# Last stage of the gated convolutions on shared weight loads, two channel groups at a time, in a new order

## The chip, the core and the metric

The kernel runs on one core of one Trainium2 chip. The metric is the device time of one execution in microseconds. Three runs of the kernel before took 241.77, 242.07 and 239.66 us, so its median is 241.77 us. One more execution was profiled; all rows quoted here come from that one.

## The reference

Two long convolutions over 2048 positions and 448 channels are mixed by a gate. `u` is the input, and both convolutions are causal (the reference takes them by FFT over the padded length).

```
x = A_u                                                   # [1, 2048, 448]
g = sigmoid(sum(x * gate_w, -1))                          # one number per position
K = Re sum_n C[d,n] * exp(dt[d] A[d,n] l) * dt[d] B[d,n]  # 2048 taps per channel, 256 modes
a = causal_conv(x, K) + x * Dskip
k_shift = 4-tap causal convolution of B_k
kv = k_shift * B_v
b = x * (causal_conv(kv, ssm_k) + kv * ssm_D)             # the gated convolution
out = g * a + (1 - g) * b
```

Inputs and output are bf16. The kernel folds both skip terms (`Dskip`, `ssm_D`) into the first tap of the convolution kernels.

## The kernel before, in words

**Layout.** The 448 channels are 4 groups of 112. A position is 64·a + b with a below 32 and b below 64, and the 128 partitions are (group, a). So a tensor in natural order is 128 partitions by 64 values of b by 112 channels. `natv` (called `vt`, later `ug`) first holds `v`, then k_shift·v, and at the end the output; `natu` (called `uu`) holds the shifted copy of `k` for the taps and then `u`, which arrives by four DMAs on the SP queue after the taps are done.

**Stages.** The 112 channels are worked in four windows H = 0..3 of 28 (`NC`). A convolution of one window is a chain of matrix products in TensorE, each leaving PSUM through ScalarE or VectorE:

- `spread` (matmuls with `Wc` or `WcK`) and `transform` (matmuls with 32 matrices of `s2_W`): the forward transform of the data and of the taps;
- `swapped`: eight DMAs on SP that exchange the two halves of the partitions of one factor, for the complex product;
- `products`: two VectorE multiplications of 128x3584;
- `stage_a` (matmuls with `R`): first stage of the inverse, evacuated as `U` of shape [2, 64, 28] into a slot;
- `stage_b` (matmuls with `G`): the last stage. For each of the 64 values of b and each of two terms r it loads a 128x128 slice of `G` and multiplies it with `U[:, r, b]`, 28 columns; the two terms add up in PSUM. 32 values of b fill one piece of two PSUM banks, which is then consumed.

**Order of calls.** `PLAN` says in which order the parts are written down. `B` is a window of the gated convolution (`conv_B`), `T` makes the taps of a window of the other one (`table`: `exps` and `levels` with exponentials and sines on ScalarE, then `tables` of VectorE products, `sums` on TensorE, `gather`, `spread`), `A` is a window of the other convolution (`conv_A`), and `m` is a VectorE pass over a finished window (`mix`). `A` of window 0 has its own `stage_b`; windows 1, 2 and 3 share one `stage_b` of 84 columns in six pieces at the end of the kernel (`epilogue`: a gated multiplication out of PSUM, an addition, the stores).

**How the last stage of a `B` window is consumed.** For windows 0, 1 and 2 `epilogue_B` multiplies each of two pieces out of PSUM with the window of `u` on VectorE and writes `ug`. For window 3 `held` copies the two pieces to `ug` by `evac`, and the pass `("m", 3)` multiplies the window with `u` afterwards. The pass `("m", 0)` adds the two finished convolutions of window 0.

**Resources.** `places.slots` are eight SBUF slots of 128x3584 bf16, handed out in the order of the digits of `SLOTS`; `places.joint(n)` hands out n at once as one tile. `places.room()` hands out one of four PSUM rooms of two banks by the digits of `ROOMS`. `evac` takes the next letter of `SIDES`: V evacuates with VectorE, S with ScalarE; there are 265 letters, 57 of them V.

**What sets the order.** All calls are recorded, 6102 of them, and `Order.issue` emits them in the order of the list `ORDER`, with an ordering dependency from each instruction to the one before it on its engine. So the order on each engine and on the SP and POOL queues is written out by hand; every recorded instruction is therefore put down to the same line, L131, of the profile, and the groups are told apart by their tiles (`q` are the slots, `ps` the PSUM rooms, `TP` and `TQ` the tables).

Of the kernel before, what the change touches and what calls it, by code (L numbers as in the profile page):

```python
# [36 lines left out]
PLAN = (("T", 0), ("B", 0), ("B", 1), ("T", 1), ("B", 2), ("A", 0), ("T", 2), ("B", 3), ("A", 1), ("T", 3), ("A", 2), ("m", 0), ("m", 3), ("A", 3))  # L37
PIECES = (12, 12, 12, 12, 12, 4)
SLOTS = (
    "0434052127765603307644115551700367426427537106156704014032"  # L40
)
ROOMS = (
    "01233232320132033030321023302112031100122001132032113022220031322311020231103030220220312330023120301132132010331031"
    "3231321320202123101203132012012212012323303012030110320011003102201222120212310132310321"
)
SIDES = (
    "SSSSVSVSVSSSSSSSSSSVVVVVVSSVSSSSVSVSSSSSSSSSSSSSSSSSSVVSSSVSSSVSSSSSVSSSSSSSSSVSSSSVVSVSVSVSVVVVVVVSSSSSSSSSSSSSSSSS"
    "SSSSSSSSSSSSSSSSSSSSSVSSSSSSSSSSVVSVSVSSVVVSSSSSSSSSSSSSSSSSSSSSSSSSSSSSSSSSSSSSSSSSSSSSSVVVVVVSVVVSVSSVVSSSVSSSVSSS"
    "SSSSSSSSSVSSSSSSSSSSSVVSSSSVSSSSV"
)  # L50
ORDER = (
# [277 lines left out]


def stage_b(nc, places, G, U, consume, less=None, pieces=(32, 32), w=NC):
    per = 512 // w if w > NC else 16
    b0 = 0
    for n in pieces:
        pt = places.room()
# [605 lines left out]
```

## Time and profile before

| what | us |
|---|---|
| median of three runs | 241.77 |
| the profiled execution, whole | 242.85 |
| its span, first to last instruction | 241.1 |
| VectorE (DVE) busy in it | 216.2 |
| ScalarE (ACT) busy in it | 195.1 |
| TensorE matmuls (PE) busy | 199.7 |
| TensorE weight loads (PEld) busy | 187.1 |

The profile's groups give busy time, the count behind an x, the mean ns of one instruction, and the idle time of the engine just before with what ended it. A busy time of matmuls counts each from its start to its modelled end, and they overlap; the mean of a matmul is therefore longer than the distance from one to the next. In the view by windows, each engine has the busy time in the stretch and the number of instructions. In the timeline a row is a run of like instructions: start, duration of the run, engine, kind, tiles, count, and in brackets the idle time before it and what ended it.

### The profile page before, as it was taken

Reading aid. Unit: us, or ns where it says so; the run is one execution under the profiler, and the core shown is the slowest. Engines: PE = TensorE matmul, PEld = TensorE weight load, DVE = VectorE, ACT = ScalarE, POOL = GpSimd, SP = SyncE. Lnnn points to the kernel's source line nnn. Section 1 sums busy time; section 2 is a strip of 40 time slices with the busy share of each in tenths; the row PEclk is TensorE's granted clock in tenths of the full one; section 3 lists DMA queues with packets and bytes.
Section 4 is the critical chain, followed back from the end, with each engine's and each line's share of the span. In section 5 each row is a group of like instructions: output and inputs, shape, how many; then the busy total and the mean of one; then the engine's idle time right before and its main releaser. Section 6 shows DMA issues by size and latency. Waiting matters only on the chain.

```text
span 241.1 us, 11786 instructions
## 1 busy us (share of the span) xinstructions
PE 199.7 (83%) x5358; PEld 187.1 (78%) x5358; DVE 216.2 (90%) x316; ACT 195.1 (81%) x260; POOL 22.2 (9%) x34
## 2 busy tenths in 40 slices
PE   1701988899978996999999999989999999799930
PEld 1501887898867996998999999989999899689720
DVE  1999999998987996999899999999999999977790
ACT  2899976998986986799999999988999998449000
POOL 9400001110000020100000012000121120000000
PEclk9999999999999999799999999999999999979995
DMA  6999999989384699641506047142175373500195
GB/s 142 217 182 203 153 185 315 194 192 203 61 141 93 158 176 218 145 96 31 127 8 120 3 79 137 21 97 63 22 155 102 79 132 94 129 5 3 34 175 98
DMA packets 64865, 28.86 MB, mean 120 GB/s; under 512 B 54960, under 2 KB 63280, under 8 KB 64688
## 3 DMA queue, kind: packets, MB, share of 16 engines
q1 hardware_dynamic: 57904, 21.69, 43.9%
q0 software_dynamic: 2160, 5.51, 12.6%
q10 hardware_dynamic: 4752, 0.92, 2.1%
q8 instruction: 42, 0.69, 1.3%
q14 instruction: 7, 0.06, 0.1%
HBM read 10.41 MB, written 2.75 MB: 55 GB/s over the span
## 4 chain that ended last, share of the span: by engine, by line
DVE 31%; PE 23%; DMA 8%; SPq 6%; issue 5%; ACT 3%; DVEq 0%
PE ps L131 23%; DVE TQ L131 11%; DVE TP L131 10%; SPq L131 6%; DVE q L131 4%; DMA natu<-in_A_u_dram 4%; ACT q L131 3%; DVE natv L131 3%; DVE natu L131 2%; DMA TP<-TP 2%; DMA q<-q 2%; DVE RK L131 1%; DVE ET L131 0%; ACT RK L131 0%; DVEq L131 0%
## 5 line engine op out<-in xcount | busy, mean ns | idle before, releaser
L131 ACT CAST q<-ps 128x1024 bf16<-128x1024 f32 (+3 forms) x158 | 132.8, 936 | 15.6 <-PE ps L131 11.2
L131 PEld LDWEIGHTS <-q 128*128 128x128 bf16 (+3 forms) x944 | 60.7, 143 | 21.6 <-DVE q L131 11.8
L131 PE MATMUL ps<-small,q 128*128 128x128 bf16 (+2 forms) x688 | 45.2, 240 | 13.3 <-DMA natv<-in_B_v_dram 11.4
L131 DVE TENSOR_TENSOR TQ<-TQ,ET 128x896 bf16<-128x896 bf16 (+2 forms) x70 | 45.8, 685 | 0.2
L131 PE MATMUL ps<-TP,TQ 128*32 128x32 bf16 x1792 | 33.9, 241 | 5.6 <-issue 3.7
L131 PEld LDWEIGHTS <-TQ 128*32 128x32 bf16 x1792 | 30.7, 155 | 8.0 <-issue 5.2
L131 PE MATMUL ps<-q,s_W 128*128 128x112 bf16 (+1 forms) x544 | 32.2, 211 | 2.3 <-DVE natv L131 1.9
L131 DVE TENSOR_TENSOR q<-q 128x3584 bf16<-128x3584 bf16 (+1 forms) x22 | 32.4, 1511 | 1.9 <-ACT q L131 0.8
L131 PEld LDWEIGHTS <-natu 128*32 128x32 bf16 (+1 forms) x560 | 28.5, 183 | 4.5 <-issue 3.8
L131 DVE TENSOR_TENSOR TP<-TP,ET 128x1792 bf16<-128x1792 bf16 (+3 forms) x25 | 31.5, 1271 | 0.0
L131 PEld LDWEIGHTS <-G 128*128 128x128 bf16 x768 | 28.7, 117 | 2.3 <-DVE q L131 0.7
L131 PEld LDWEIGHTS <-s_W 128*128 128x128 bf16 x544 | 26.9, 98 | 4.7 <-issue 3.0
L131 PE MATMUL ps<-q,G 128*128 128x28 bf16 (+1 forms) x768 | 29.9, 186 | 0.5 <-ACT q L131 0.5
L131 POOL DMA_DIRECT2D TP<-TP x15 | 13.1, 893 | 147.3 <-issue 41.6
L131 ACT ACTIVATE q<-hold 128x448 bf16<-128x448 f32 (+1 forms) x48 | 22.7, 534 | 0.1
L131 ACT ACTIVATE ET<-q 128x1344 bf16<-128x1344 int16 (+1 forms) x12 | 17.5, 1469 | 0.1
L131 PE MATMUL ps<-q,natu 128*32 128x336 bf16 (+3 forms) x336 | 15.0, 289 | 2.4 <-ACT q L131 2.1
L131 ACT CAST RK<-ps 128x448 bf16<-128x448 f32 (+1 forms) x16 | 12.0, 762 | 6.0 <-PE ps L131 6.0
L131 DVE CAST q<-ps 128x896 bf16<-128x896 f32 (+4 forms) x14 | 12.8, 918 | 3.5 <-PE ps L131 3.3
L131 PE MATMUL ps<-small,natu 128*64 128x128 bf16 x224 | 15.5, 284 | 0.3 <-DVE natv L131 0.3
L131 PE MATMUL ps<-small,natv 128*64 128x128 bf16 x224 | 15.2, 285 | 0.3 <-ACT q L131 0.3
L131 DVE TENSOR_TENSOR TQ<-TQ 128x448 bf16<-128x448 bf16 (+2 forms) x35 | 15.3, 445 | 0.1
(63 smaller groups left out, 197.5 us busy)
## 6 DMA issues: line engine op xcount, KB each, us to landing
q<-q SPq DMA_DIRECT2D x64, 112.0 KB, 3.4
TP<-TP POOLq DMA_DIRECT2D x9, 448.0 KB, 5.7
q<-in_B_ssm_k_dram SPq DMA_DIRECT2D x16, 112.0 KB, 3.8
natv<-in_B_v_dram SPq DMA_DIRECT2D x4, 448.0 KB, 7.3
natu<-in_A_u_dram SPq DMA_DIRECT2D x4, 448.0 KB, 6.9
TP<-TP POOLq DMA_DIRECT2D x6, 224.0 KB, 4.5
s_W<-c_W SPq DMA_DIRECT2D x1, 1024.0 KB, 6.5
G<-c_G SPq DMA_DIRECT2D x4, 256.0 KB, 5.2
```

What stands on the lines that cost most here:

```text
L131: ins = f(*args, **kw)
```

## The change

- `conv_B` no longer ends in its own `stage_b`. An even window takes two slots as one tile (`places.joint(2)`), and `inverse` writes its `U` into the first half; the odd window writes the second half, and then one `stage_b` serves both windows: 64 values of b times two terms, 56 columns each, in four pieces of 16 values of b.
- `epilogue_B` now takes each piece of both windows: it multiplies 2 x 8 x 56 columns out of PSUM with `u` and writes `ug`, for windows (0, 1) and (2, 3) alike. `held` and the pass `("m", 3)` are gone.
- `per` in `stage_b` is rounded down to an even number (8 for 56 columns; 84 columns keep 6).
- `ORDER`, `SLOTS`, `ROOMS` and `SIDES` are new throughout. There are 5845 calls (256 fewer matmuls and one pass fewer); `SIDES` has 263 letters, 54 of them V.

```diff
-PLAN = (..., ("A", 2), ("m", 0), ("m", 3), ("A", 3))
+PLAN = (..., ("A", 2), ("m", 0), ("A", 3))
 ...
 def stage_b(nc, places, G, U, consume, less=None, pieces=(32, 32), w=NC):
-    per = 512 // w if w > NC else 16
+    per = 512 // w // 2 * 2 if w > NC else 16
 ...
-    def epilogue_B(H):
-        def consume(b0, n, pt):
-            o = window(ug, b0, n, H).rearrange("p (i b) c -> p i b c", b=16)
-            x = window(uu, b0, n, H).rearrange("p (i b) c -> p i b c", b=16)
-            V.tensor_tensor(out=o, in0=pt.rearrange("p i (b c) -> p i b c", b=16), in1=x, op=ALU.mult)
-        return consume
-
-    def held(t, H):
-        def consume(b0, n, pt):
-            evac(window(t, b0, n, H).rearrange("p (i b) c -> p i b c", b=16), pt.rearrange("p i (b c) -> p i b c", b=16))
-        return consume
+    def epilogue_B(b0, n, pt, H):
+        o, x = (t[:, b0:b0 + n, H * NC:(H + 2) * NC].rearrange("p (i b) c -> p i b c", i=2) for t in (ug, uu))
+        V.tensor_tensor(out=o, in0=pt.rearrange("p i (b c) -> p i b c", c=2 * NC), in1=x, op=ALU.mult)
 ...
+    pair = []
+
     def conv_B(H):
 ...
-        conv(products(nc, K, S, X), epilogue_B(H) if H < NQG - 1 else held(ug, H))
+        terms = products(nc, K, S, X)
+        if H % 2 == 0:
+            pair.append(places.joint(2).rearrange("p h (r b c) -> p h r b c", r=2, b=64))
+        inverse(pair[-1][:, H % 2], terms)
+        if H % 2:
+            U = pair[-1]
+            stage_b(nc, places, G, lambda r, b: U[:, :, r, b], lambda b0, n, pt: epilogue_B(b0, n, pt, H - 1), None, (16,) * 4, 2 * NC)
 ...
-        V.tensor_tensor(out=o, in0=o, in1=x, op=ALU.mult if H else ALU.add)
+        V.tensor_tensor(out=o, in0=o, in1=x, op=ALU.add)
```

The new `ORDER` also moves work that the change does not touch. On VectorE the two products of `A` window 1 and the pass `("m", 0)` stand behind the last of the `tables` instructions now, and stood ahead of it. On SP the eight swaps of `B` window 1 stand ahead of all four loads of `u`; before, two of these loads stood ahead of the swaps and two behind them. On ScalarE three of window 2's sine passes stand between its exponentials now; before, they stood ahead of them.

More of the change, by code (lines that the diff above doesn't have):

```diff
@@ L36 @@
 NSLOT = 8
-PLAN = (("T", 0), ("B", 0), ("B", 1), ("T", 1), ("B", 2), ("A", 0), ("T", 2), ("B", 3), ("A", 1), ("T", 3), ("A", 2), ("m", 0), ("m", 3), ("A", 3))
+PLAN = (("T", 0), ("B", 0), ("B", 1), ("T", 1), ("B", 2), ("A", 0), ("T", 2), ("B", 3), ("A", 1), ("T", 3), ("A", 2), ("m", 0), ("A", 3))
 PIECES = (12, 12, 12, 12, 12, 4)
 SLOTS = (
-    "0434052127765603307644115551700367426427537106156704014032"
+    "0410735562045402302751323214026032471666553507656744714032"
 )
 ROOMS = (
-    "01233232320132033030321023302112031100122001132032113022220031322311020231103030220220312330023120301132132010331031"
-    "3231321320202123101203132012012212012323303012030110320011003102201222120212310132310321"
+    "10323210022103031313223213113030130032021113302022131210020033201030102011022311031022311322113002011230212303213131"
+    "1211020111123310003322233202012211013101110020323203020011123120312301233130303220313202"
 )
 SIDES = (
-    "SSSSVSVSVSSSSSSSSSSVVVVVVSSVSSSSVSVSSSSSSSSSSSSSSSSSSVVSSSVSSSVSSSSSVSSSSSSSSSVSSSSVVSVSVSVSVVVVVVVSSSSSSSSSSSSSSSSS"
-    "SSSSSSSSSSSSSSSSSSSSSVSSSSSSSSSSVVSVSVSSVVVSSSSSSSSSSSSSSSSSSSSSSSSSSSSSSSSSSSSSSSSSSSSSSVVVVVVSVVVSVSSVVSSSVSSSVSSS"
-    "SSSSSSSSSVSSSSSSSSSSSVVSSSSVSSSSV"
+    "VVSVSSVSVSSSSSSSSSSSSSVVVVSVVVSSSSVSSSSSSSSSSSSSSSSSSSVSSSSSSSSSSSSSVVVSSSSSSSVSSSSVVVVVVSSSSVSSVVSSSSSSSSSSSSSSSSSS"
+    "SSSSSSSSSSSSSSSSSVSSSSSSSSSVVVSVVVVVVSSVVVSSSSSSSSSSSSSSSSSSSSSSVSSSSSSSSSSSSSSSSSSVSSVSSSSSVSSVSVSSVSSSSSSSVSVSSSSS"
+    "SSSSSSSSSSSSSSSSSSSSVSVSVSSSVVS"
 )
 ORDER = (
[46 rows of a table removed]
[46 rows of a table added]
 )
```

92 rows, old and new, of the table ORDER are left out of this document.

## The prediction

> **What bounds the kernel now.** I read the page first, then busy time by stretches, then the waits of VectorE, then the timelines at the places where VectorE stood still, and last the groups by shape.
>
> ```profile
> span 241.1 us, 11786 instructions
> PE 199.7 (83%) x5358; PEld 187.1 (78%) x5358; DVE 216.2 (90%) x316; ACT 195.1 (81%) x260; POOL 22.2 (9%) x34
> ...
> core 0: us, PE busy (x) PEld busy (x) DVE busy (x) ACT busy (x) POOL busy (x), PEclk, DMA share, GB/s
> 0.00:20.00 20.00, 4.98 (x48) 4.45 (x48) 14.34 (x24) 14.32 (x23) 8.29 (x17) 1.00 0.89 180
> 20.00:55.00 35.00, 29.10 (x712) 27.45 (x712) 34.43 (x50) 30.48 (x43) 2.72 (x3) 1.00 1.05 208
> 55.00:116.00 61.00, 55.19 (x1517) 51.95 (x1517) 54.53 (x69) 52.65 (x68) 2.60 (x3) 0.97 0.68 133
> 116.00:205.00 89.00, 86.61 (x2478) 81.55 (x2470) 87.79 (x145) 86.23 (x116) 8.57 (x11) 1.00 0.40 81
> 205.00:235.00 30.00, 23.85 (x624) 21.67 (x624) 25.14 (x31) 11.44 (x16) 0.00 (x0) 0.94 0.33 69
> ...
> 98.00:198.00 100.00, 97.13 (x2753) 92.13 (x2754) 97.99 (x152) 97.51 (x132) 8.57 (x11) 1.00 0.40 83
> ```
>
> VectorE is the bound. From 20 to 55 us it lacks 0.6 us, from 116 to 205 us 1.2 us. It is idle only from 55 to 116 (6.5 us) and in the tail from 205 (4.9 us). ScalarE is as full as VectorE from 98 to 198. TensorE looks as full, but its busy time holds overlapped latencies, as the pricing below shows. Who makes VectorE wait between 55 and 116:
>
> ```profile
> DVE natv L131 <- DMA natu<-in_A_u_dram: 2.6, 1, 2.6
> DVE TQ L131 <- PE ps L131: 2.4, 2, 2.2
> ...
> 73.86 0.62 DVE L131 TENSOR_TENSOR TQ<-hold,ET 128x896 bf16<-128x896 bf16 x1 [2.25 <-PE ps L131]
> ...
> 92.66 2.09 DVE L131 TENSOR_TENSOR natv<-ps,natu 128x896 bf16<-128x896 f32 x2 [2.59 <-DMA natu<-in_A_u_dram]
> ...
> 203.39 1.83 DVE L131 TENSOR_TENSOR TQ<-TQ,ET 128x448 bf16<-128x448 bf16 x5
> ...
> 234.32 0.68 DVE L131 TENSOR_TENSOR natv<-natu,natv 128x1008 bf16<-128x1008 bf16 x1
> ```
>
> Two holes hold 4.8 of the 6.5 us: at 71.6 the first table product of window 1 waits for TensorE to finish reading the tables of window 0, and at 90.1 the last stage of `B` window 0 waits for `u`. The last two rows mark the tail: the last table instruction ends at 205.2, the last VectorE instruction at 235.0. The span then needs 6.1 us for the stores.
>
> **The change part by part.** Everything is priced by these groups:
>
> ```profile
> L131 ACT CAST q<-ps 128x896 bf16<-128x896 f32 x64 | 56.1, 933 | 10.3 <-PE ps L131 6.7 <-DVE natv L131 3.5
> ...
> L131 DVE TENSOR_TENSOR q<-q 128x3584 bf16<-128x3584 bf16 x14 | 27.9, 2019 | 1.7 <-ACT q L131 0.8 <-issue 0.5 <-DVE q L131 0.3
> ...
> L131 PE MATMUL ps<-q,G 128*128 128x28 bf16 x640 | 23.3, 183 | 0.0
> ...
> L131 PE MATMUL ps<-q,G 128*128 128x84 bf16 x128 | 6.6, 201 | 0.5 <-ACT q L131 0.5
> ...
> L131 DVE TENSOR_TENSOR natv<-ps,natu 128x896 bf16<-128x896 f32 x6 | 6.4, 1086 | 2.6 <-DMA natu<-in_A_u_dram 2.6
> ...
> L131 ACT ACTIVATE q<-hold 128x224 int32<-128x224 f32 x16 | 6.1, 415 | 0.0
> L131 DVE TENSOR_SCALAR q<-hold 128x224 int32<-128x224 f32 x23 | 6.0, 306 | 0.0
> ...
> L131 DVE CAST q<-ps 128x896 bf16<-128x896 f32 x4 | 4.3, 1081 | 0.1
> ...
> L131 DVE TENSOR_TENSOR natv<-natv,natu 128x1792 bf16<-128x1792 bf16 x2 | 2.2, 1086 | 0.0
> ...
> L131 ACT CAST natv<-ps 128x896 bf16<-128x896 f32 x2 | 2.0, 1019 | 0.0
> ...
> L131 ACT ACTIVATE ET<-ET 128x672 bf16<-128x672 bf16 x2 | 1.6, 790 | 0.5 <-DVE ET L131 0.5
> ...
> L131 ACT COPY q<-ps 128x224 f32<-128x224 f32 x4 | 1.2, 335 | 0.0
> ```
>
> *TensorE.* Today a last-stage matmul of 28 columns with its weight load costs 23.3/640 = 36.4 ns of busy time, one of 84 columns 6.6/128 = 51.6 ns. Shape 56 is not in the trace, and lies halfway: between 36.4 and 51.6, I take 44. Before, 512 x 36.4 = 18.6 us; after, 256 x 44 = 11.3 us. TensorE loses 7.4 us (5.4 to 9.3). Since it is not the bound, this does not shorten the path by itself; it only lets TensorE be ready earlier. A price of twice 36.4, at which nothing is shared, is excluded by the row of 84 columns.
>
> *VectorE.* Two windows now leave by four products of 896 out of PSUM; over the kernel there are eight instead of six, +2 x 1.09, and the pass over window 3 goes, -1.09: +1.1 us. The writes go to 56 adjacent columns instead of 28; I keep 1.09.
>
> *ScalarE.* The two copies of window 3 go, -2.0 us.
>
> *The letters.* I laid the letters of `SIDES`, old and new, beside the calls that take them. Until the end of the tables VectorE gets two transforms (2 x 1.08) and two short copies, and gives away two casts of `spread` and `stage_a`, five phases and two negations; successive VectorE instructions overlap by about 0.08 us, and net of that it is some -0.7 us. Behind the tables it gets three casts (two of `stage_a`, one of `gather`) and gives one away: +2.0. ScalarE loses four large casts in all, the two of window 3 among them (4 x 0.95 = -3.8), and two short copies (-0.7), and gets the five phases (5 x 0.42 = +2.1) and two negations (2 x 0.79 = +1.6): -0.8 us.
>
> *A cost that the diff does not name.* ScalarE reloads its function table whenever exponentials and sines alternate:
>
> ```profile
> L131 ACT ACT_TABLE_LOAD x6 | 7.7, 1283 | 1.3 <-PEq L925 1.2
> ...
> 158.62 1.28 ACT L131 ACT_TABLE_LOAD   x1
> 159.91 1.32 ACT L131 ACTIVATE ET<-q 128x1344 bf16<-128x1344 int16 x1
> ```
>
> The new order puts window 2's three sine passes between its exponentials, so there are eight loads instead of six: +2 x 1.28 = +2.6 us, right in the stretch where ScalarE has 2.5 us left in 100. Nothing hides them there. ScalarE ends at -0.8 + 2.6 = +1.8 us. (The Trainium skill, "ScalarE: Activation LUTs", section "What ACT_TABLE_LOAD costs", adds a drain of about 1.38 us to each switch; by it the two would cost 5.3 us. The trace differs: the sine starts 0.01 us behind the load, so the row decides.)
>
> *The end of the tables.* Ahead of that point VectorE loses the products of `A` window 1 (2 x 2.0 less overlap, -3.9) and the pass over window 0 (-1.0 net), both moved behind it, gains two last-stage products (+2.0 net) and loses 0.7 by letters: -3.6 us. These 3.9 and 1.0 are only moved.
>
> *The hole at 90.1.* What the SP queue does before it:
>
> ```profile
> 77.47 4.51 SPq L131 DMA_DIRECT2D q<-q  x6
> 82.02 3.22 SPq L131 DMA_DIRECT2D natu<-in_A_u_dram  x2
> ```
>
> The last loads of `u` are issued at 82 to 85 because six swaps of `B` window 1 stand ahead and wait for that window's transforms, which TensorE reaches late. In the new order these transforms are early, the swaps follow those of window 0 directly, and the first consumer of `u` on VectorE stands some 9 us of VectorE work later. I take the full 2.6 us as gained (0 if the swaps, whose last pieces wait for a cast on VectorE, hold the queue again).
>
> *The hole at 71.6.* Between the end of window 0's tables and the last read of them, TensorE has three runs of eight `transform` matmuls fewer in the new order,
>
> ```profile
> 85.98 0.57 PE L131 MATMUL ps<-q,s_W 128*128 128x112 bf16 x8
> ```
>
> at up to 0.57 us each, so up to 1.7 us; VectorE has 0.4 us more of its own work in the same stretch. Of the hole 0 to 2.1 us are gained; I take the middle, 1.1.
>
> *New waits.* One is visible, in the second half of window 3's tables:
>
> ```profile
> 192.44 2.08 DVE L131 TENSOR_TENSOR TP<-TP,ET 128x1792 bf16<-128x1792 bf16 x2
> ...
> 201.09 1.08 DVE L131 TENSOR_TENSOR TP<-TP,q 128x1792 bf16<-128x1792 bf16 x1
> ```
>
> The second row needs what a DMA on the POOL queue sums up behind the first, and starts 6.6 us after it ends; in the new order 4.2 us of VectorE work lie between the two. I put 0.6 us (0 to 1.5, as the wait need not show at all or may take most of the missing 2.4). One slot of eight is held from window 2's `stage_a` to window 3's last stage; whatever waits for slots I cannot price and leave to the range.
>
> *The tail.* Its 25.1 us of VectorE work gain the two products (+3.9), the casts (+2.0) and the pass over window 0, and lose the pass over window 3: 31.1. Some of the 4.9 us idle is filled by this, the chain sums, `gather`, `spread`, transform, product, `stage_a` still has to run: between 31.1 and 36.0, I take 33, +3.0.
>
> *Sum*, against the profiled execution: 242.85 - 3.6 - 2.6 - 1.1 + 0.6 + 3.0 = 239.15, which is -3.7 us. The runs' median lies 1.1 us under that execution: 241.77 - 3.7 = **238.1 us**. With all bounds at their good end -3.6 - 2.6 - 2.1 + 1.1 = -7.2 (234.6); all at the bad end, -3.6 + 1.5 + 6.0 = +3.9 (245.7); they hardly meet all at one end, and 234.5 to 241.5 is this case's own range.
>
> **Rivals.**
>
> *No change: the evacuating engines set the pace.* VectorE's total rises (1.1 - 0.7 + 2.0 = 2.4 us) and ScalarE's by 1.8. If closed holes reappear as waits elsewhere and only the one for `u` stays closed, 241.77 + 2.4 - 2.6 = 241.6; with none closed 244.2. For it: 97.99 and 97.51 of 100 us. Against: 11 us of idle time are there to be taken. (The Trainium skill, "Perfetto Trace Analysis", section "Identifying the Most-Contended Engine", says to work on the engine with the highest occupancy and not to trust matmul busy time; here that is VectorE with 90%, and the change takes nothing from it. The trace agrees as to matmul time.)
>
> *TensorE was the bound after all.* It is also busy 97.13 of those 100 us. Then the 7.4 us come off whole: 234.4. Against: 36 ns per matmul where one lasts 183.
>
> *Slower: results wait for VectorE in PSUM.* Two of eight pieces could leave by ScalarE before; now all need VectorE, in its written order, and each keeps one of four rooms until then:
>
> ```profile
> 82.97 2.29 PE L131 MATMUL ps<-q,G 128*128 128x28 bf16 x64
> ```
>
> This piece was complete at 85.3 and stood until 92.66: 7.4 us. If TensorE runs out of rooms because of it, ScalarE runs dry with it, and has no slack to catch up. At one instruction of 1.09 us per piece, eight pieces cost 8.7 us: 238.1 + 8.7 = 246.8. It decides from the fourth blocked piece on, where the 3.7 us are eaten. For it: four pieces at once need all four rooms. Against: the new order puts other matmuls between the pieces.
>
> **Chances and range.** Forecast case 0.50, no change 0.22, TensorE 0.10, slower 0.18. About 1% is what a measurement of this kernel tells from none: 239.35 and 244.2. The forecast case lies below 239.35 in 0.40 and within in 0.10; TensorE adds 0.10 to faster; no change gives 0.03, 0.17 and 0.02; slower gives 0.02 within and 0.16 above. Faster 0.53, same 0.29, slower 0.18. The range 232 to 245 leaves out a part of the TensorE case and most of the slower one.
>
> **What would show it.** 256 matmuls of 56 columns at 36 to 52 ns busy each; eight VectorE rows of 896 out of PSUM and none of ScalarE into `natv`; eight table loads; the row `DVE natv <- DMA natu` gone; the last table instruction near 198.5 instead of 205.2; some 33 us from there to VectorE's end. I am wrong if VectorE's idle time between 98 and 198 grows by more than 2 us (slower), if the tail takes over 36 us, or if the tables end no earlier.

## The result, and the profile after

The changed kernel took 247.88 us (median of four runs, 247.09 to 250.17) against 241.05 us for the kernel before, a ratio of 1.029 with a 95% interval of 1.021 to 1.037. The prediction was 238.1 us: the sign was wrong. Measured a second time beside some of the experiments below, the changed kernel's median was 248.49 us (four executions, 244.71 to 253.88), so a few microseconds between two medians are near the spread of one kernel. The profiled execution took 250.17 us, 2.3 us over the median; its absolute times carry that.

From the page of the changed kernel: span, busy time, and the granted TensorE clock in 40 equal slices.

```profile
span 248.4 us, 11277 instructions
...
PE 194.7 (78%) x5102; PEld 179.3 (72%) x5102; DVE 218.2 (88%) x314; ACT 197.3 (79%) x263; POOL 22.2 (9%) x34
...
PEclk9999689999997999997999799995999999999995
```

The same clock row of the kernel before:

```profile
PEclk9999999999999999799999999999999999979995
```

VectorE does 2.0 us more work than before and ScalarE 2.2 us; both numbers were forecast nearly so. But the span is 7.3 us longer, so VectorE stands idle more. Where, is seen in the view by windows of the changed kernel (busy time and, behind the x, instructions of each engine; then granted clock, DMA share, GB/s):

```profile
20.00:55.00 35.00, 24.93 (x618) 22.62 (x613) 29.34 (x46) 22.96 (x31) 1.90 (x2) 0.90 0.95 173
55.00:116.00 61.00, 55.64 (x1505) 52.18 (x1507) 58.88 (x72) 57.90 (x77) 3.44 (x4) 0.94 0.76 148
116.00:205.00 89.00, 77.28 (x2147) 71.90 (x2140) 81.41 (x135) 83.27 (x108) 8.42 (x11) 0.94 0.36 74
...
98.00:198.00 100.00, 86.47 (x2335) 81.10 (x2334) 93.29 (x142) 93.26 (x123) 8.42 (x11) 0.93 0.35 73
```

The middle stretch is better than before: VectorE is busy 58.88 of the 61 us from 55 to 116, and was 54.53. The loss lies on both sides of it. From 20 to 55 VectorE lacks 5.7 us where it lacked 0.6, and from 116 to 205 it lacks 7.6 where it lacked 1.2. Between 98 and 198 its idle time went from 2.0 to 6.7 us, more than the 2 us by which the prediction had said it would be wrong.

The groups by shape that price the change itself (busy time, mean ns of one | idle time before them):

```profile
L131 ACT ACT_TABLE_LOAD x8 | 10.3, 1283 | 1.6 <-PEq L925 1.2 <-DVE q L131 0.3
L131 PE MATMUL ps<-q,G 128*128 128x56 bf16 x256 | 9.8, 194 | 1.0 <-DVE natv L131 1.0
L131 DVE TENSOR_TENSOR natv<-ps,natu 128x896 bf16<-128x896 f32 x8 | 8.5, 1082 | 0.0
...
L131 PE MATMUL ps<-q,G 128*128 128x28 bf16 x128 | 5.1, 182 | 0.0
```

The last stages of `B` now cost 38 ns of busy time per matmul (9.8/256), and with the rest of the 28-column ones these groups keep TensorE busy 8.4 us less (23.3 before, 9.8 + 5.1 now). TensorE's busy time as a whole fell by 5.0 us only (199.7 to 194.7). VectorE's waits in the whole kernel (idle time, how often, the longest):

```profile
DVE q L131 <- DMA q<-q: 3.9, 2, 3.2
DVE natv L131 <- ACT q L131: 3.7, 2, 3.2
DVE q L131 <- PE ps L131: 3.5, 3, 1.8
DVE TQ L131 <- PE ps L131: 2.3, 2, 1.6
DVE TP L131 <- DMA TP<-TP: 1.3, 1, 1.3
```

The row for `u` is gone, and the product of window 1's tables with `hold` waits 1.6 us where it waited 2.2. In their place stand waits that the trace of before does not have. Of the three largest, two lie in the start, in the taps (at 47.02 and 52.17), and one at 163.44 (VectorE's timeline):

```profile
27.16 0.28 DVE L131 TENSOR_TENSOR q<-q,dB 128x28 bf16<-128x28 bf16 x1
...
47.02 0.63 DVE L131 TENSOR_TENSOR natv<-q,natv 128x896 bf16<-128x896 bf16 x1 [3.19 <-ACT q L131]
...
52.17 1.09 DVE L131 CAST q<-ps 128x896 bf16<-128x896 f32 x1 [1.81 <-PE ps L131]
...
163.44 3.96 DVE L131 TENSOR_TENSOR q<-q 128x3584 bf16<-128x3584 bf16 x2 [3.23 <-DMA q<-q]
...
204.86 1.09 DVE L131 TENSOR_TENSOR TP<-TP,q 128x1792 bf16<-128x1792 bf16 x1 [1.25 <-DMA TP<-TP]
...
207.17 1.53 DVE L131 TENSOR_TENSOR TQ<-TQ,ET 128x448 bf16<-128x448 bf16 x4
...
242.19 0.68 DVE L131 TENSOR_TENSOR natv<-natu,natv 128x1008 bf16<-128x1008 bf16 x1
```

and TensorE's timeline at the same place:

```profile
27.50 2.35 PE L131 MATMUL ps<-small,q 128*64 128x128 bf16 x40 [4.82 <-DVE q L131]
...
45.31 0.40 PE L131 MATMUL ps<-q,natu 128*32 128x336 bf16 x2 [3.40 <-issue]
```

At 27.16 VectorE adds `dB` (the skip term of window 1 of `B`) to that window's convolution taps, an instruction of 0.28 us that stands behind five others in VectorE's written order. The first `spread` of that window reads the sum, and TensorE, which in the new order has this `spread` ahead of the taps, stands still 4.82 us for it. The taps then start late, and at 41.9 TensorE stops again for 3.40 us that the profile puts down to no other engine ("issue"); the last section shows that such a stop is a wait for TensorE's own instructions. A second profiled execution of the changed kernel (`a0_after`) has the 4.82 us too, and two such stops of 2.13 and 3.10 us in the taps, where this one has 3.40 and 1.72. Where VectorE's time went in all, summed from its rows in the timeline (stretches end with the last table instruction of a window, T0 to T3, and with VectorE's last instruction):

| VectorE's idle time, us | before | after | after, with the addition moved (`s1_add_up`) |
|---|---|---|---|
| start to T0 | 6.7 | 11.4 | 7.5 |
| T0 to T1 | 5.2 | 1.7 | 2.2 |
| T1 to T3 | 2.0 | 8.0 | 4.5 |
| T3 to the end (the tail) | 4.9 | 3.6 | 5.5 |
| T3 ends at | 205.2 | 208.7 | 201.9 |
| work until T3 | 191.3 | 187.6 | 187.7 |
| VectorE ends at | 235.0 | 242.9 | 238.2 |
| work in all | 216.2 | 218.2 | 218.4 |

So the forecast's 3.6 us of work do leave the time ahead of T3, and 3.5 us of the holes between T0 and T1 do close. They are eaten by +4.7 us at the start and +6.0 us between T1 and T3. The third column belongs to an experiment.

### The profile page after: what moved, and what is told of

The parts are those of the page before. It is cut to its first block, busy times and chain, and to the rows that moved or that the text cites. A ratio compares the mean times of both kernels' runs of the same rounds, so it can differ in the third digit from the quotient of the medians.

```text
span 248.4 us, 11277 instructions
## 1 busy us (share of the span) xinstructions
PE 194.7 (78%) x5102; PEld 179.3 (72%) x5102; DVE 218.2 (88%) x314; ACT 197.3 (79%) x263; POOL 22.2 (9%) x34
## 4 chain that ended last, share of the span: by engine, by line
PE 26%; DVE 23%; ACT 18%; SPq 14%; DMA 9%; issue 6%; POOL 0%; DVEq 0%; POOLq 0%
PE ps L131 26%; ACT q L131 15%; SPq L131 14%; DVE q L131 10%; DMA q<-q 5%; DVE TQ L131 4%; DVE TP L131 3%; ACT ET L131 3%; DMA G<-c_G 3%; DVE natu L131 2%; DVE natv L131 2%; DVE ET L131 1%; DMA q<-in_B_ssm_k_dram 1%; DMA small<-c_Wc 1%; ACT L131 1%
## 5 line engine op out<-in xcount | busy, mean ns | idle before, releaser
L131 ACT CAST q<-ps 128x896 bf16<-128x896 f32 (+4 forms) x157 | 132.8, 935 | 20.6 <-PE ps L131 19.5
L131 PEld LDWEIGHTS <-q 128*128 128x128 bf16 (+3 forms) x944 | 62.4, 146 | 30.8 <-DVE q L131 18.2
L131 PE MATMUL ps<-small,q 128*128 128x128 bf16 (+2 forms) x688 | 47.5, 247 | 20.7 <-DVE q L131 17.2
L131 PE MATMUL ps<-TP,TQ 128*32 128x32 bf16 x1792 | 33.4, 241 | 7.8 <-issue 4.5
L131 ACT ACTIVATE q<-hold 128x448 bf16<-128x448 f32 (+1 forms) x52 | 24.8, 520 | 1.5 <-DVE q L131 1.4
L131 PEld LDWEIGHTS <-G 128*128 128x128 bf16 x512 | 20.3, 116 | 3.8 <-issue 1.2
L131 PE MATMUL ps<-q,G 128*128 128x56 bf16 (+2 forms) x512 | 21.6, 193 | 1.8 <-DVE natv L131 1.0
L131 PE MATMUL ps<-q,natu 128*32 128x336 bf16 (+3 forms) x336 | 15.8, 303 | 5.1 <-issue 5.1
L131 DVE CAST q<-ps 128x896 bf16<-128x896 f32 (+4 forms) x15 | 13.8, 939 | 3.6 <-PE ps L131 3.5
L131 PE MATMUL ps<-q 128*32 128x336 bf16 (+3 forms) x112 | 15.7, 303 | 0.0
L131 PE MATMUL ps<-small,natu 128*64 128x128 bf16 x224 | 14.5, 283 | 0.3 <-ACT q L131 0.3
```

The source lines that it names most:

```text
L131: ins = f(*args, **kw)
```

## The experiments

Four questions: what the start costs, what the sharing is worth, what pairing does without the new order, and whether clock or table loads explain the rest. Ratios are to the kernel before, run beside each experiment, with 95% intervals. In diffs of lists, numbers are calls.

**The start.** First I put the first thousand calls back into the old order, with the old letters for them:

```diff
-ORDER = <the new list>
+ORDER = <the calls of the new list's first part, in their old sequence; then the rest of the new list>
```

> The changed kernel, with its first 1000 of 5845 instructions (up to some 62 us) put back into the order and the letters of the kernel before; the paired last stage and the rest of the new order stay. Order theory: VectorE's idle time between 40 and 55 us, 5.5 us in the changed kernel, falls under 1 us, and 3.5 to 5 us of it reach the end: 243 to 244.5 us instead of 247.9. Rival, the time gained early is given back at the next waits (tables of window 1, u): 246.5 to 248 us.

Measured 252.31 us, 1.046 (1.032 to 1.059): not better. VectorE's waits only changed their places, 1.4, 1.3, 0.9, 2.4 and 3.0 us between 34 and 66 us, since the rest of the list was still written for the new start. Undoing less, I put only window 1's load and first `spread` of `B` behind the taps:

```diff
-ORDER = "... <load and first spread of B 1> ... <taps> ..."
+ORDER = "... <taps, with load and first spread of B 1 among the last of them> ..."
```

> The changed kernel with one block moved: the load and the first spread of B window 1 (4 DMAs, one addition, 56 matmuls and their 4 evacuations) go from ahead of the tap matmuls to behind the last of them. If the stall between 22 and 52 us (TensorE idle 4.8 us at 27.5 for that load's addition, granted clock 0.65 from 25 to 35, taps late) carries to the end: VectorE's idle time at 47 to 52 us falls from 5.5 to under 2.5 us and the time from 247.9 to 243.5 to 246. Rival, the block is needed just behind the taps and only changes places: 247 to 250 us.

251.75 us, 1.041 (1.031 to 1.050). The wait went to the next consumer, VectorE's cast of that window's transform:

```profile
54.90 1.09 DVE L132 CAST q<-ps 128x896 bf16<-128x896 f32 x1 [6.37 <-ACT q L132]
```

Nor did it help to write the lists around the start anew, from the durations of the traces, with that block behind the taps (16 letters change), or to do the same for the kernel before with only windows 0 and 1 paired (20 letters; that kernel is described below):

```diff
-ORDER, SLOTS, ROOMS, SIDES = <as given>
+ORDER, SLOTS, ROOMS, SIDES = <calls up to some 105 us (r2) or from 20 to 125 us (r3) listed by earliest start with the trace's durations>
```

> The changed kernel with the load and spread of B window 1 behind the taps, and its lists replanned up to what ran at 105 us (16 letters change too); behind that the changed kernel's own order. If the stall between 22 and 57 us is what its start costs, the tables of window 0 end at 58 to 60 us instead of 64 and those of window 1 at 106 to 109 instead of 112, and the time falls to 242 to 246 us from 248. Rival, the late stretch takes it back: 247 to 251 us.

> Windows 0 and 1 paired as in the first of these, with the lists replanned from 20 to 125 us (20 letters change). If an order planned from durations can better the one of the kernel before: 234 to 239 us, under both kernels. Rival, what such a plan doesn't know (late instruction fetches, half clock, crowded DMA) makes it worse than the mended one: 243 to 252 us.

255.29 us, 1.048 (1.026 to 1.069), and 256.42 us, 1.065 (1.052 to 1.078). In both VectorE then waits for `v` in the first tap product, 4.79 us at 37.35 and 6.16 us at 38.78. I take it that durations from one trace do not hold when the transfers meet in another order; no run shows this by itself. What worked was to move one instruction:

```diff
-ORDER = "... 717 715 738 114 739 74 6 1403 1353-1369 115 1618 745 1616 1619 720 ..."
+ORDER = "... 717 715 1618 1616 1619 738 114 739 74 6 1403 1353-1369 115 745 720 ..."
```

On VectorE only the addition of `dB` changes its place, five instructions ahead.

> The changed kernel with one VectorE instruction moved: the 0.28 us addition of B window 1's load, for which TensorE stands from 22.7 to 27.5 us ahead of all taps, goes from 27.2 to about 24.7 us (its load has landed at 24.2). If TensorE's late taps are the start's stall: the taps begin 2 to 3 us earlier, VectorE's waits at 47 to 52 us shrink by as much, and 2 to 3 us reach the end: 245 to 246.5 us against 248. Rival, the taps are held by the loads, the instruction fetches and VectorE's list anyway: 247 to 249.5 us.

244.37 us (ten runs, 242.72 to 246.14), 1.016 (1.009 to 1.023): 3.5 us less than the changed kernel by the medians and 3.1 by the ratios, about half of its loss. The two intervals overlap a little (1.021 and 1.023), so the place of this loss is surer than its size. The timeline of this kernel, first TensorE's, then VectorE's:

```profile
25.79 2.34 PE L132 MATMUL ps<-small,q 128*64 128x128 bf16 x40 [2.39 <-ACT q L132]
...
40.19 0.39 PE L132 MATMUL ps<-q,natu 128*32 128x336 bf16 x2 [0.91 <-issue]
```

```profile
25.45 0.28 DVE L132 TENSOR_TENSOR q<-q,dB 128x28 bf16<-128x28 bf16 x1
...
46.23 0.62 DVE L132 TENSOR_TENSOR natv<-q,natv 128x896 bf16<-128x896 bf16 x1 [0.56 <-ACT q L132]
...
48.39 1.09 DVE L132 CAST q<-ps 128x896 bf16<-128x896 f32 x1 [0.46 <-PE ps L132]
```

The addition comes 1.71 us earlier, TensorE starts 1.71 us earlier, and its stop is 2.39 us instead of the 4.82 that both executions of the changed kernel have. Behind it, more went than these 1.7 us: the stop of 3.40 us shrank to 0.91, and VectorE's waits of 3.19 and 1.81 to 0.56 and 0.46. Start to T0 now holds 7.5 us of idle time, and held 11.4.

**The clock.** After the first stop the granted clock is low. The view by windows, first of the changed kernel, then of the one with the addition moved:

```profile
25.00:30.00 5.00, 2.50 (x44) 2.33 (x48) 5.00 (x13) 3.27 (x6) 0.00 (x0) 0.65 1.17 173
30.00:35.00 5.00, 5.00 (x120) 4.05 (x120) 4.93 (x8) 3.02 (x6) 0.00 (x0) 0.66 1.37 162
```

```profile
25.00:30.00 5.00, 4.21 (x84) 3.68 (x88) 5.00 (x12) 4.99 (x8) 0.00 (x0) 1.00 1.14 194
30.00:35.00 5.00, 5.00 (x168) 4.84 (x161) 4.93 (x9) 3.32 (x4) 0.00 (x0) 1.00 1.25 156
```

From 30 to 35 us TensorE issues 120 matmuls instead of 168. The 1.00 from 25 to 30 us must not be taken at its word: the view counts the clock as full where nothing is recorded, and the first record of this trace is at 29.2 us. The 40 `spread` matmuls at 25.79 took 2.34 us, as long as the 2.35 us of those in the changed kernel, and 1.31 us in `s2_add_up_fill` below, where full clock is on record at that time. So between 25 and 35 us the clock at which the two kernels work differs from 29.2 to 33.4 us alone. To see whether the clock by itself is the cause, I filled TensorE's pauses with matmuls of 256 columns whose results nobody reads: 159 of them in six pauses of the changed kernel, 18 in the pause that is left with the addition moved, and 70 ahead of the first `spread` of the kernel before.

```diff
+FILL = {1370: 45, 1671: 50, 2458: 12, 2850: 14, 4099: 26, 4974: 12}
 ...
-            for f, args, kw in self.calls[int(a):int(b or a) + 1]:
+            for j, (f, args, kw) in enumerate(self.calls[int(a):int(b or a) + 1], int(a)):
+                for _ in range(FILL.get(j, 0)):
+                    fill = self.tc.nc.tensor.matmul(<the room that the next call writes>, lhsT=self.fill[0], rhs=self.fill[1], start=True, stop=True)
```

> The changed kernel in its own order and letters, with 159 extra matmuls (identity times 256 constant columns, into the room that the next real matmul overwrites) put on TensorE where it stands idle: 45 ahead of its first spread (12 to 19 us), 50 ahead of the spread of B window 1 (gap at 22.7 to 27.5), 12 ahead of the sums of window 1 (110.8), 14 ahead of the stage_a of B window 2 (125.7), 26 ahead of that of B window 3 (164 to 167.5) and 12 ahead of the sums of window 3 (207). They compute nothing. Clock theory (stretches of 3.4 us in which TensorE was mostly idle are followed by 3.4 us at half clock, seven such in the changed kernel ahead of 235 us, two in the kernel before; that is where the 6 to 7 us went): half-clock stretches fall from 5 to 7 to at most 3, the time from 248 to 241 to 244.5 us, in spite of the added work. Rival, the pauses themselves are the loss and the clock only follows them: 247 to 252 us.

> The same with 18 matmuls that compute nothing in what is left of that pause (22.7 to 24.9 us), so that the clock is not halved from 26 to 33 us as in the changed kernel. If the half clock is what makes the taps late: no stretch of it between 23 and 40 us, tables of window 0 done by 61 us instead of 64, 243.5 to 245.5 us. Rival: within 1.5 us of the run without the filling.

> The kernel before, with 70 such matmuls ahead of its first spread, where TensorE is idle from 11.5 to 22.9 us. Its clock counts as low until 27.2 us in the kernel before; with them it is up at 22.9. Clock theory: up to 2 us of TensorE time gained in the taps, 239 to 241.5 us beside 241.5 to 242. Rival: 241.5 to 243 us.

The mean clock of the changed kernel rose from 0.938 to 0.978, and its time to 255.00 us, 1.058 (1.050 to 1.065). The others took 251.27 us (too scattered for a ratio) and 245.64 us, 1.012 (1.001 to 1.022). But the mean clock rose in the first alone: it was 0.935 with the 18 filling matmuls and 0.958 without them, and 0.976 in the kernel before with its 70 and 0.974 without. And in the changed kernel the fill ahead of window 1's `spread` itself ran until 32.9 us, ahead of the taps, which it pushed back, so for the start these runs do not tell what the clock costs. Behind the start the comparison is cleaner. From T0 to T3, first the changed kernel, then the same with the fill:

```profile
63.92:208.71 144.79, 126.56 (x3570) 117.84 (x3570) 135.04 (x200) 135.96 (x179) 11.00 (x14) 0.94 0.51 101
```

```profile
66.86:211.06 144.20, 130.61 (x3634) 121.40 (x3634) 134.94 (x201) 135.97 (x180) 10.92 (x14) 0.99 0.51 101
```

With the clock at 0.99 instead of 0.94 the stretch is 0.6 us shorter, and VectorE still stands idle 9.3 us of it (9.7 without the fill, 7.2 in the kernel before). So far as this pair shows (64 of the filling matmuls lie in its pauses), the clock does not explain these waits.

**What the sharing is worth.** Everything of the change stays, but each matmul of 56 columns is two of 28, each with its own weight load; once in all windows, and once in windows 2 and 3 alone:

```diff
-                for r in range(2):
-                    nc.tensor.matmul(o ..., lhsT=G[...], rhs=U(r, b0 + i0 + i), ...)
+                for x, r in [(x, r) for x in range(2 if w == 2 * NC else 1) for r in range(2)]:
+                    u = U(r, b0 + i0 + i)
+                    nc.tensor.matmul(o[:, x * NC:(x + 1) * NC] ..., lhsT=G[...], rhs=u[:, x] ..., ...)
```

> The changed kernel in its own order, letters and buffers; only each 56-column matmul of the paired last stage is issued as two of 28 columns, each with its own weight load (256 matmuls and weight loads more). Order theory (TensorE is off the path, the loss of the change sits in where the new order puts its waits): TensorE works some 5 to 7 us more, the time stays within 1.5 us of the changed kernel's 247.9 us, 247 to 249.5. Rival, TensorE sets the pace in the new order: 253 to 255 us.

> The changed kernel, with the weight loads unshared for windows 2 and 3 alone (128 matmuls more). If TensorE paces throughout: half of the 7.4 us of the full unsharing, 251 to 252.5 us. If only the place of windows 0 and 1 counts: 247.5 to 249; if only that of 2 and 3: 254 to 255.5 us.

255.26 us, 1.058 (1.047 to 1.069), and 252.64 us, 1.046 (1.037 to 1.056). One of the four executions of the first, the profiled one, took 362.58 us and is not in the ratio; the others took 254.23 to 256.02, their median is 254.5. So taking back the 8.4 us of TensorE time (the price comes from the groups above, since this trace is of the odd execution) costs 6.6 us of the whole by the medians and 7.0 by the ratios (1.058 against 1.029); half of it costs 4 to 5 (against 247.88 or 248.49). The counterpart in the old order: the kernel before, with the first matmul of each sum in the last stages of `B` issued twice, 256 matmuls more:

```diff
-                for r in range(2):
+                for r, once in ((0, True), (0, False), (1, False)) if w == NC and less is None else ((0, False), (1, False)):
```

> The kernel before, in its own order, with the first matmul of each last-stage sum of the B windows issued twice (256 matmuls of 28 columns and their weight loads more, some 8 us of TensorE; the result is the same). If TensorE sets the pace in the old order as the unshared run showed for the new one: 248 to 250 us. Rival, TensorE has slack in the old order (VectorE is the bound): 241 to 243.5 us.

247.29 us, 1.022 (1.011 to 1.032). The group grew from 23.3 us:

```profile
L132 PE MATMUL ps<-q,G 128*128 128x28 bf16 x896 | 31.8, 183 | 0.0
```

8.5 us more of busy TensorE cost 0.022 x 241 = 5.2 us, with an interval of 2.7 to 7.7. Last, both versions with all lists written anew by one method (earliest start with the trace's durations), so that neither keeps a list that was worked out for the other:

```diff
-ORDER, SLOTS, ROOMS, SIDES = <as given>
+ORDER, SLOTS, ROOMS, SIDES = <the same calls, listed anew>
```

> The changed kernel with the same instructions, but all four lists (order, letters, slots, rooms) replanned from the durations of the two traces, with TensorE's tap stage taken up to half longer than in its undisturbed stretches, so that no engine's list rests on taps that come on time. If the loss of the change is one of its order: under the kernel before, 232 to 239 us. Rival, the paired structure costs by itself (one slot less, four products at once): 243 to 249 us.

> The kernel before (last stage of the B windows one at a time), its lists replanned in the same way. It has 256 more matmuls in its last stages than the paired one. If TensorE's time counts in a good order too: 2 to 5 us slower than the paired one planned in the same way, 234 to 242 us; if pairing only costs: faster than that one by 3 us or more.

> The replanned paired kernel with each 56-column matmul issued as two of 28 columns with their own weight loads, nothing else changed (256 matmuls more). If the 7.4 us that unsharing cost in the changed kernel's order were TensorE's pace: 5 to 8 us slower than the replanned paired kernel. Rival, there they were a late list made later: 0 to 3 us slower.

Paired and shared 255.17 us, 1.052 (1.041 to 1.062); the instructions of before 262.74 us, 1.078 (1.066 to 1.090); paired but unshared 261.91 us, 1.080 (1.069 to 1.090). In these lists, too, sharing is worth 6.7 us (1.080 against 1.052). The pairing and the products from PSUM show no price of their own, 1.080 against 1.078; but these two lists differ in more than that (`SIDES` has 69 letters V in the paired one and 63 in the other), so it is not shown that there is none. All three are worse than both given kernels, so this method finds no better order.

**Pairing in the old order.** The kernel before, its lists nearly untouched, with only windows 0 and 1 of `B` paired:

```diff
-        conv(products(nc, K, S, X), epilogue_B(H) if H < NQG - 1 else held(ug, H))
+        terms = products(nc, K, S, X)
+        if H > 1:
+            conv(terms, epilogue_B(H) if H < NQG - 1 else held(ug, H))
+            return
+        if H == 0:
+            pair.append(places.joint(2).rearrange("p h (r b c) -> p h r b c", r=2, b=64))
+        inverse(pair[0][:, H], terms)
+        if H == 1:
+            stage_b(nc, places, G, lambda r, b: pair[0][:, :, r, b], epilogue_pair, None, (16,) * 4, 2 * NC)
```

> The kernel before, in its own order and letters, with the paired last stage for windows 0 and 1 alone (windows 2 and 3 as before): 128 matmuls of 56 columns instead of 256 of 28, and the first products of window 0 move from 92 us to where window 1's stand. Order theory (the paired structure costs nothing by itself): the hole of 2.6 us at 90 us goes, 238 to 241 us against 241 of the kernel before. Rival, the structure itself costs (results wait longer in PSUM, VectorE gets them later and in bunches): 242.5 to 246 us.

247.14 us, 1.024 (1.013 to 1.034). The timeline of this kernel, first VectorE's, then TensorE's:

```profile
92.36 2.03 DVE L132 TENSOR_TENSOR TP<-TP,ET 128x3584 bf16<-128x3584 bf16 x1 [2.97 <-DMA TP<-TP]
...
108.10 1.09 DVE L132 TENSOR_TENSOR natv<-ps,natu 128x896 bf16<-128x896 f32 x1 [2.81 <-PE ps L132]
...
110.93 2.03 DVE L132 TENSOR_TENSOR q<-gw,small 128x3584 bf16<-128x3584 bf16 x1 [1.74 <-PE ps L132]
```

```profile
105.35 1.15 PE L132 MATMUL ps<-q,s_W 128*128 128x112 bf16 x16 [3.65 <-DVE natv L132]
```

Here the rival of the PSUM rooms is seen: TensorE cannot start its next transforms for 3.65 us, because the pieces of the paired stage hold rooms until VectorE takes them, and VectorE then waits for those transforms. In the changed kernel TensorE waits 1.0 us in all for `natv` on VectorE, 5.4 in this one: there the order keeps the rooms free. Writing the lists from 88 to 125 us anew (order, slots and rooms; letters unchanged) mends part of it:

```diff
-ORDER = "... <88 to 125 us of the paired kernel> ..."
+ORDER = "... <the same calls, listed by earliest start> ..."
```

> The run with windows 0 and 1 paired in the old order, its lists replanned in one stretch only (what ran from 88 to 125 us; letters unchanged): the waits that the pairing left there on VectorE (3.0 us for the accumulating DMA at 92, 1.0 and 2.8 for the paired products at 101 and 108, 1.7 for the gate's slot at 111) get other work in front of them. If these list places are the whole cost of pairing: 5 us or more of them go, 238 to 242 us against 247.1 unmended and 241 to 242 for the kernel before. Rival, the paired structure costs by itself: 245 to 248 us.

244.68 us, 1.018 (1.005 to 1.030). VectorE's idle time until T1 fell by 6.0 us (17.2 to 11.2), but the median by 2.5: new waits of 1.70 us at 121.02 and 1.25 us at 167.81, both products that wait for swaps, took 3.6 of it back by T3.

**The table loads.** In the changed list, window 2's sine passes were put ahead of its exponentials again:

```diff
-ORDER = "... <exponential> <sines> <exponential> ..."
+ORDER = "... <sines> <exponentials> ..."
```

> The changed kernel, with window 2's three sine passes ahead of all its exponentials: six function-table loads instead of eight (and the phases of these passes on VectorE 1 to 8 us earlier). If ScalarE sets the pace from 95 to 165 us in the new order: the wait of the products of B window 3 at 163 us (3.3 us) shrinks by 2 us or more, and the time falls from 247.9 to 245 to 246.5 us. Rival, the loads fall into waits that are there anyway: 247.3 to 248.5 us.

251.24 us, 1.043 (1.032 to 1.054), but it doesn't test what it was meant to. Its group of table loads, and then the fifth of them in ScalarE's timeline:

```profile
L131 ACT ACT_TABLE_LOAD x8 | 10.3, 1283 | 1.4 <-PEq L925 1.2 <-DVE q L131 0.2
```

```profile
99.96 1.28 ACT L131 ACT_TABLE_LOAD   x1
```

The load that went away with the exponentials came back at 99.96 us for the gate's activation, which had shared the exponentials' table. With eight loads as before, and the nine exponentials in one row, VectorE waited 2.14 us for them at 126.12. What two loads fewer would be worth stays open.

**The changed kernel again.**

> The changed kernel as it is, on the same chip as the variants beside it: 247 to 250 us, and the same waits at 47, 52, 79 and 163 us.

248.49 us, as told above. Its profiled execution ends T3 at 207.1 us with 18.0 us of idle time; the wait of 3.23 us at 163.44 is not in it, the one for the POOL queue is (1.75 us). So the single waits between T1 and T3 differ between executions, and their sum (5.7 us here) less so.

## Why the prediction was wrong

The sum was -3.6 - 2.6 - 1.1 + 0.6 + 3.0 us. Two of its steps failed and turned the sign. It put nothing for the start, and VectorE's idle time there grew by 4.7 us; it put 0.6 us for new waits, and between T1 and T3 they grew by 6.0. Work ahead of T3 and the holes came out as forecast, and the tail's idle time fell by 1.3 us where 3.0 had been counted on. By its own steps:

*The end of the tables, -3.6.* Right as work: 187.6 us until T3 instead of 191.3. Wrong as time: T3 ends at 208.7, not near 198.5. With the addition moved it is 201.9, 3.3 us earlier than before: this term, and nothing of the holes.

*The holes at 90.1 and 71.6, -2.6 and -1.1.* The first closed as said: the row for `u` is gone. The second did not close, and its reading was incomplete: the wait fell from 2.25 to 1.57 us, and a stop of TensorE for its own instructions lies in it both times, 1.19 us until 72.05 before and 1.50 us until 77.64 now. Between T0 and T1 idle time fell by 3.5 us (forecast 3.7). That this shortens the path was the error. In `s1_add_up` the 3.0 us saved there come back as 2.5 us of small waits between T1 and T3 (1.23 us for a product of `A` window 0, 0.84 and 0.69 for phases and tables) and 0.8 at the start. Here the time went as in the rival "no change", by which closed holes reappear elsewhere, "with none closed 244.2": 244.37 us measured, though for another order than the forecast one, so that the agreement to 0.2 us is luck. In the changed kernel as given it is 6.0 us that come back between T1 and T3.

*The wait in the second half of window 3's tables, +0.6.* 1.25 us in the first profiled execution, within 0 to 1.5; 1.75 in the second, and none in `s1_add_up`.

*The tail, +3.0.* 34.2 and 33.6 us in the two executions of the changed kernel, 36.3 in `s1_add_up`, forecast 33 within 31.1 to 36. Its work was right (30.6 for 31.1), its idle time was taken too low (3.0 to 5.5 instead of 1.9). I take it that the chain of the last window does not shorten because VectorE has more to do beside it; that is not shown.

*What was not in the sum at all.* The start was left unread. The prediction looked at the letters, at SP's order around `u` and at the stretch from 55 on; the stretch from 20 to 55, where VectorE lacked 0.6 us, it took as unchanged, though `ORDER` is new throughout. The hoisted `spread` of window 1 makes TensorE wait for an addition of 0.28 us, and that costs 3.1 to 3.5 us, as `s1_add_up` shows. With the addition moved, the kernel still stands 3.3 us above the kernel before.

*"Since it is not the bound, this does not shorten the path by itself."* This step fails too, but in the other direction: it left out a gain. 8.4 us less of busy TensorE are worth 6.6 to 7.0 us in the new order (`e1_unshared`), 6.7 in lists written anew, and 8.5 us more cost 5.2 (2.7 to 7.7) in the old order. So a microsecond of busy TensorE counts 0.6 to 0.8 here, although VectorE is the busiest engine. This price holds more than the matmuls: with the added instructions TensorE's stops for its own instructions grew as well, from 9.6 to 13.0 us in the lists written anew and from 4.3 to 6.5 in the old order. (The Trainium skill, "Perfetto Trace Analysis", section "Identifying the Most-Contended Engine", warns off matmul busy time as a measure of roofline. As the price of work taken off, which that section does not speak of, the busy time came close here.) A chain passes through three engines in turn in every window, and in the kernel before all three are full, 97.99, 97.51 and 97.13 of 100 us. I conclude that each of them is a bound somewhere.

*The rivals.* "TensorE was the bound after all" was right about the price and wrong about the time; it has to be added to everything else. The PSUM rooms were wrong here and right in the old order.

**What stays open.** With sharing taken out, the new order costs 13 to 14 us against the kernel before (1.058) at about the same TensorE work. Of that, the start is 3.1 to 3.5 (shown) and VectorE's added work 2.0 to 2.2 (counted). The other 8 us are waits spread over the windows, which none of the rewritten lists took away. How much of them TensorE's stops for instructions make, 4.3 us in all before and 10.2 and 10.7 in the two executions of the changed kernel, is open: they are 9.7 in `s1_add_up`, which is 3.5 us faster, and 3.7 in `e5_b1later`, which is slower. It is open, too, why the block of instructions for the 3.40 us stop came late. TensorE had passed the block before it at 37.7 us, and its transfer began at 43.0; other transfers filled the 16 DMA engines to 96.6% in between. No version beat the kernel before; the best were 244.37 (`s1_add_up`) and 244.68 us (`r1_pair01_mended`).

## What to carry to other kernels

When the order of all engines is written out and all are above 95% busy in the same stretch, work taken off any of them can count, and waits that close on one can come back on another; price all of them by taking work off or adding it, not by which is busiest. A new order has to be read from its first instruction on: look, for each hoisted group, at what its first instruction reads and where the producer stands in its engine's order. A small late instruction (0.28 us here) can cost more than ten times its length, and moving it alone is the cheapest experiment.

## What the runs showed of the hardware

- The granted clock falls to 0.50 for stretches of about 3.4 us or twice that, and short pauses are enough: in the changed kernel a pause from 76.1 to 77.6 us was followed by such a stretch from 77.7 to 81.1. Over nineteen traces (the 362.58 us execution has no such records, and the last fall of each, at its end, is left out), 77 of 82 falls came after 3.4 us in which TensorE was busy 0.72 or less; but only about half of such stretches at full clock, 75 of 139, were followed by a fall. (The Trainium skill, "TensorE: Matmul & The Clock Gate", section "What's actually happening", puts the return to half clock after at least one idle window of about 3.4 us; here the pause was 1.5 us.) In the kernel with doubled 28-column matmuls a fall at 86.4 us followed a stretch in which TensorE had no pause at all.
- A 56-column matmul with its weight load takes 38 ns of busy time (9.8/256), one of 28 columns 36 to 40 (23.3/640 before, 5.1/128 now). Twice the columns cost almost nothing; the forecast had taken 44.
- TensorE's own instructions arrive as transfers on a queue of their own, in blocks of 16 KB: 40 in the changed kernel with its 2 x 5102 matmuls and weight loads, 42 in the kernel before with 2 x 5358. That makes 64 bytes for one and 256 of them in a block. From the page of the changed kernel, packets, MB and share of the DMA engines' time:

```profile
q8 instruction: 40, 0.66, 1.2%
```

  A late block stops TensorE. Its idle time that waits for nothing else ("issue": in all, times, longest) grew; first the kernel before, then the changed kernel:

```profile
PE ps L131 <- issue: 4.3, 8, 1.2
```

```profile
PE ps L131 <- issue: 10.2, 11, 3.4
```

  The nineteen traces other than that of the 362.58 us execution hold 93 such stops of 0.7 us or more. Counted through TensorE's matmuls and weight loads, every one of the 93 stands at the same place of a block of 256 (number 193 or 194, as a record can be missing), and every one ends 1.2 to 1.8 us after a 16 KB transfer of this queue has landed. The 3.40 us stop ends at 45.31, its block landed at 43.95.
